# Decode attention on one core: keys in 64 KB rows, a copy on Pool, exponentials in three parts

## The chip, the cores and the metric

The kernel runs on one core of one Trainium2 chip. The time is the device time of one execution in microseconds (us), taken as the median of several runs. The engines are named as the profile does: PE (TensorE, matrix products and transposes), DVE (VectorE), ACT (ScalarE), POOL (GpSimd) and SP (SyncE, which issues most DMA here). PEld is PE's loading of the stationary operand.

## The reference

Two attention layers decode one token for four batch rows. Their outputs stand side by side in the result.

```python
def _A_ref(x, k_cache, v_cache, wq, wo):       # 32 query heads, 8 key/value heads, last 2048 keys only
    W = min(4096, max(256, Sk // 4))           # Sk = 8192, so W = 2048
    q = (x @ wq).reshape(B, Sq, Hq, Dh).transpose(0, 2, 1, 3)
    k = jnp.repeat(k_cache[:, :, Sk - W:, :], rep, axis=1)
    v = jnp.repeat(v_cache[:, :, Sk - W:, :], rep, axis=1)
    p = softmax(einsum("bhqd,bhkd->bhqk", q, k) * Dh ** -0.5)
    o = einsum("bhqk,bhkd->bhqd", p, v)
    return o.transpose(0, 2, 1, 3).reshape(B, Sq, Hq * Dh) @ wo

# _B_ref is the same with 32 key/value heads and all 8192 keys
return concatenate([A, B], axis=-1)            # B = 4, Sq = 1, D = 512, Dh = 128, bfloat16
```

Layer B reads 4 x 32 x 8192 x 128 keys and as many values, 268 MB each. Layer A reads 33.6 MB of keys and values. There is one query per head, so nearly all of the work is to bring the caches in and to pass each key and value through PE once.

## The kernel before

Layer A is done in 8 chunks, then layer B in 32. A B chunk is one batch row and four heads: 256 tiles of 128 keys, 8.4 MB of keys and as many of values. A partition holds 64 KB of a chunk's keys (and 64 KB of its values), contiguous in memory.

On-chip buffers for these lie in one tensor of ten slots of 16 KB per partition. In layer B the keys use slots 0 to 3 and the values slots 4 to 7.

```python
kv = sb("kv", [P, NH, 8192], BF16)              # NH = 10 slots
wol = kv[:, 8, 0:4 * DO].rearrange("p (u n) -> p u n", u=4)
QK = (0, 4, 8, 16, 24)                          # transpose groups that wait for keys
QV = (0, 16, 24, 28, 30, 31)                    # product groups that wait for values
```

Keys come in two halves (32 KB a partition), values in one load, and the last chunks in smaller pieces. A load waits for what reads its slots: a key slot for the last transpose of its quarter, a value slot for the last product. SP issues the loads in this order. Pool waits for each landing and raises a counter (`relay`), on which PE waits.

```python
def dma_B(kind, c, part=None):
    ...
    if kind == "k":
        pieces, fam = (LASTK, "d_lk") if c == NC - 1 else (NEXTK, "d_nk") if c == NC - 2 else ((NTB // 2,) * 2, "d_bk")
    else:
        pieces, fam = (LASTV, "d_lv") if c == NC - 1 else (NEXTV, "d_nv") if c in (NC - 2, NC - 3) else ((NTB,), "d_bv")
    ...
    for i, n in enumerate(pieces):
        waits = []
        for u in range(j0 // unit, (j0 + n - 1) // unit + 1):
            waits += held[at + u]
            used[at + u] = [("T", ch["s"] + (u + 1) * unit // TG - 1) if kind == "k" else ("pv", c)]
        x = slice(j0 * P, (j0 + n) * P)
        sch.add_dma("sp", lambda e, x=x: e.dma_start(dst[:, x], src[:, x]), fam + str(i), waits=waits, key=(kind, c, i))
        j0 += n
        sch.relay("pool", sems, "r_" + kind, n // TG, [(kind, c, i)] + ...)

for c in range(NCA, NC):
    if (c - NCA) % NB == 0:
        dma_B("k", c, 0)
        dma_wos((c - NCA) // NB)                # 0.5 MB of the output weights, every fourth chunk
        dma_B("k", c, 1)
    else:
        dma_B("k", c)
    dma_B("v", c)
```

PE works through a B chunk in three stages. First, 32 groups of 8 tiles are transposed into PSUM (`emit_T`), copied to SBUF by DVE or ACT (22 and 10 groups) and multiplied with the query (`emit_S`). Then come the row maximum and the exponentials, during which PE reorders output weights and runs some dummy products (`keep_busy`). Last, the values are multiplied with the exponentials (`emit_pv`), which ends with the scaling on DVE (`norm_out`).

```python
def exp_B(c):
    for h in range(2):                          # two halves of the keys, four heads each
        for u, pp in HEADS:
            src = sc[pp, h, :].rearrange("p (j u) -> p u j", u=4)[:, u, :]
            dst = probs_of(c)[pp, h * NTB // 2:(h + 1) * NTB // 2, u]
            sch.add("act", lambda e, ...: e.activation(dst, src, ACTF.Exp, bias=negb[pp, 0, u:u + 1], scale=scale), ...)

def whole_B(c):
    emit_qb(c)                                  # DVE copies the chunk's four query columns
    for g in range(ch["NG"]):
        emit_T(ch["s"] + g)
        if g == 1:
            emit_fin(p)                         # output product of the chunk before
        if g >= SLAG:
            emit_S(ch["s"] + g - SLAG)
        ...
    stats_rowmax(c, 1)
    reorder(c, 0, 0)
    reorder(c, 1, 1)
    reorder(c, 2, 2)
    keep_busy(2)
    stats_gmax(c)
    keep_busy(1)
    stats_bc(c)
    exp_B(c)
    for u in range(3):
        take_wol(c, u, u)
    keep_busy(3)
    reorder(c, 3, 0)
    keep_busy(5)
    take_wol(c, 3, 0)
    sums_B(c)
    for g in range(ch["NG"]):
        emit_pv(c, g)
        ...
    norm_out(c)
```

A dummy product is a 128x128 by 128x512 matmul into `po` that nothing reads.

Of the kernel before, what the change touches and what calls it, by code (L numbers as in the profile page):

```python
# [8 lines left out]
AX = mybir.AxisListType  # L9
BF16 = mybir.dt.bfloat16  # L10
F32 = mybir.dt.float32

P = 128
TG = 8
# [154 lines left out]
def bass_concat_heads__sliding_block_cached__mha_block_cached__decode_kernel(  # L169
# [45 lines left out]
    with ExitStack() as es:  # L215
# [51 lines left out]
        semnames += ["d_h%d" % i for i in range(NH)] + ["d_bk0", "d_bk1", "d_bv0"]  # L267
        semnames += [f + str(i) for f, x in (("d_lk", LASTK), ("d_nk", NEXTK), ("d_lv", LASTV), ("d_nv", NEXTV)) for i in range(len(x))]
        semnames += ["d_wo%d" % i for i in range(NWO)] + ["d_wos"]
        sems = {n: es.enter_context(nc.semaphore(n)) for n in semnames}  # L270

# [88 lines left out]
            src = T[:, ch["g"], SkA - W:, :].rearrange("b (pp j) d -> pp b (j d)", pp=P // NB)  # L360
            sch.add_dma("sp", lambda e: e.dma_start(kv[:, at, :], src), "d_h%d" % at, waits=waits, key=(kind, c))

        def dma_B(kind, c, part=None):


            ch = chunks[c]
            T, at, steps = (B_k, KB, QK) if kind == "k" else (B_v, VB, QV)
            src = T[ch["b"], 4 * ch["hq"]:4 * ch["hq"] + 4].rearrange("u (pp j) d -> (u pp) (j d)", pp=P // 4)
            dst = flat(at, 4)
            if kind == "k":  # L370
                pieces, fam = (LASTK, "d_lk") if c == NC - 1 else (NEXTK, "d_nk") if c == NC - 2 else ((NTB // 2,) * 2, "d_bk")
            else:
                pieces, fam = (LASTV, "d_lv") if c == NC - 1 else (NEXTV, "d_nv") if c in (NC - 2, NC - 3) else ((NTB,), "d_bv")
            j0, unit, used = 0, NTB // 4, {}
            for i, n in enumerate(pieces):
                if part is not None and i != part:
                    j0 += n
                    continue
                waits = []
                for u in range(j0 // unit, (j0 + n - 1) // unit + 1):  # L380
                    waits += held[at + u]
                    used[at + u] = [("T", ch["s"] + (u + 1) * unit // TG - 1) if kind == "k" else ("pv", c)]
                x = slice(j0 * P, (j0 + n) * P)
                sch.add_dma("sp", lambda e, x=x: e.dma_start(dst[:, x], src[:, x]), fam + str(i), waits=waits, key=(kind, c, i))
                j0 += n
                sch.relay("pool", sems, "r_" + kind, n // TG, [(kind, c, i)] + ([("wos", ch["hq"])] if i == 1 and kind == "k" and ch["b"] == 0 else []))
            for g, end in zip(steps, steps[1:] + (NTB // TG,)):
                sch.tk[(kind + "r", c, g)] = ("r_" + kind, (c - NCA) * (NTB // TG) + end)
            for u in used:
                held[u] = used[u]  # L390

        KB, VB = 0, 4

        dma_x(0)
        dma_x(1)
# [6 lines left out]
            dma_A("v", c)  # L402
            dma_wo(c)
        for c in range(NCA, NC):
            if (c - NCA) % NB == 0:
                dma_B("k", c, 0)
                dma_wos((c - NCA) // NB)
                dma_B("k", c, 1)
            else:
                dma_B("k", c)  # L410
            dma_B("v", c)

        ms_read = []
        po_read = []
# [42 lines left out]


        def tile_of(kind, c, j):
            at = half_of[(kind, c)] if c < NCA else KB if kind == "k" else VB  # L460
            return flat(at, chunks[c]["NT"] // NTA)[:, j * P:(j + 1) * P]

        bank_used = [None] * NTRB
# [1 line left out]
        def emit_T(s):  # L465
            c, g = groups[s]
            bank = g % NTRB
            if c == NCA and g == 0:
                bank_used[:] = [None] * NTRB
            before, bank_used[bank] = bank_used[bank], s  # L470
            for t in range(TG):
                waits = []
                if t == 0:
                    if c >= NCA:
                        waits = [("kr", c, g)] if g in QK else []
# [115 lines left out]
        def probs_of(c):  # L591
            ch = chunks[c]
            return pbt[ch["ab"]][:, par(c), 0:ch["NT"] * ch["UC"]].rearrange("p (j x) -> p j x", x=ch["UC"])

        def exp_B(c):
            pw = [("c_pb", 1)] + ([("pv", c - 1), ("rs", c - 1)] if c > NCA else [])
            for h in range(2):
                for u, pp in HEADS:
                    src = sc[pp, h, :].rearrange("p (j u) -> p u j", u=4)[:, u, :]
                    dst = probs_of(c)[pp, h * NTB // 2:(h + 1) * NTB // 2, u]  # L600
                    sch.add("act", lambda e, src=src, dst=dst, pp=pp, u=u: e.activation(dst, src, ACTF.Exp, bias=negb[pp, 0, u:u + 1], scale=scale),  # L601
                            waits=[("negb", c)] + pw if u == h == 0 else [], key=("exp", c, h) if u == 3 else None)
                sc_read[h] = [("exp", c, h)]

        def sums_B(c):
            sch.add("dve", lambda e: e.tensor_reduce(out=rst[1][:, :], in_=probs_of(c).rearrange("p j u -> p u j"), axis=AX.X, op=ALU.add),  # L606
                    waits=[("exp", c, 1)] + rs_read[NSM], key=("rs", c))

        def shift_A(c):
            C = chunks[c]["C"]  # L610
# [185 lines left out]
        def whole_B(c):  # L796


            ch, p = chunks[c], prev(c)
            sch.mark()  # L800
            emit_qb(c)
# [116 lines left out]
```

## Time and profile before

| what | before |
|---|---|
| time, median of 3 runs | 1372.56 us (1372.38 to 1374.11) |
| span of the profiled run | 1371.8 us |
| PE busy | 1249.8 us (91%) |
| DVE busy | 744.0 us (54%) |
| ACT busy | 513.8 us (37%) |
| POOL busy | 9.8 us (1%), all at the start |
| read from memory | 587.21 MB |
| granted PE clock over the span | 0.981 |
| transposes `tr<-identb,kv` | 8704 |
| evictions `kt<-tr` on DVE | 736, mean 691 ns |
| exponentials `pbb<-sc,negb` | 256, mean 538 ns |
| dummy products `po<-sel,identb` | 352 |

Busy time of an engine is a share of the whole span and says little of what ends a wait. In the timeline a row gives the start, the duration, the engine, the line, the operation with its shapes and how often it was repeated; the bracket gives the idle time of that engine just before and what ended it. "POOLq" in a bracket stands for Pool's instruction queue, that is, the counter that Pool raises after a landing. A DMA share of 1.00 means that the packets took as much time as 16 engines have.

### The profile page before, as it was taken

The page shows a single profiled execution, that of the slowest core. Times are in us where ns is not written, and L with a number is a line of the kernel's source. Part 1 is how long each engine was busy: PE and PEld are TensorE (multiplying, and loading weights), DVE is VectorE, ACT ScalarE, POOL GpSimd, SP SyncE. Part 2 cuts the span into 40 slices and gives each one's busy share as a digit, 9 for nine tenths or more (in the row PEclk, how much of TensorE's full clock was granted, in tenths as well). Part 3 has the DMA queues.
Part 4 walks back from the last instruction along what each step waited for, and adds up shares of the span by engine and source line. Part 5 has one row for each costly group of instructions (what it writes and reads, how often), then busy time and mean ns, then how long its engine had stood idle before and what let it go on. Part 6 is the DMA issues. An engine that isn't in the chain of part 4 may idle for free.

```text
span 1371.8 us, 61526 instructions
## 1 busy us (share of the span) xinstructions
PE 1249.8 (91%) x27769; PEld 1110.4 (81%) x27769; DVE 744.0 (54%) x1335; ACT 513.8 (37%) x649; POOL 9.8 (1%) x29
## 2 busy tenths in 40 slices
PE   4897999998999999999999999999999999998998
PEld 4786788888778787888777888888778889877887
DVE  1675456655545556555555555554555555554555
ACT  1553244433333344333333443333333433333333
POOL 2000000000000000000000000000000000000000
PEclk9998899999999999999999999999999999999999
DMA  9999999999999999999999999999999999999998
GB/s 398 427 426 444 417 422 431 432 437 441 428 438 428 423 434 434 431 438 440 428 428 424 438 431 429 445 432 428 434 429 429 430 438 438 434 430 429 422 428 340
DMA packets 21084, 587.52 MB, mean 428 GB/s; under 512 B 2356, under 2 KB 2376, under 8 KB 4808
## 3 DMA queue, kind: packets, MB, share of 16 engines
q1 hardware_dynamic: 21032, 587.21, 99.6%
q8 instruction: 15, 0.25, 0.1%
q14 instruction: 5, 0.04, 0.0%
q10 hardware_dynamic: 32, 0.01, 0.0%
HBM read 587.21 MB, written 0.01 MB: 428 GB/s over the span
## 4 chain that ended last, share of the span: by engine, by line
DMA 57%; PE 39%; DVE 2%; issue 1%; ACT 0%; SPq 0%; POOLq 0%; DVEq 0%
DMA kv<-in_B_k_cache_dram 36%; DMA kv<-in_B_v_cache_dram 18%; PE tr L419 18%; PE po L421 9%; PE sc L421 8%; DMA kv<-in_B_wq_dram 2%; PE fin L421 1%; PE ms L421 1%; PE tr L421 1%; DMA kv<-in_A_k_cache_dram 1%; DVE sA L539 1%; DVE kt L486 0%; DVE kv L716 0%; ACT pba L623 0%; DVE rm L551 0%
## 5 line engine op out<-in xcount | busy, mean ns | idle before, releaser
L419 PE MATMUL tr<-identb,kv 128*128 128x128 bf16 x8704 | 668.6, 221 | 48.2 <-POOLq L72 42.3
L486 DVE COPY kt<-tr 128x1024 bf16<-128x1024 bf16 x736 | 501.9, 691 | 264.0 <-PE tr L419 261.3
L484 ACT ACTIVATE kt<-tr 128x1024 bf16<-128x1024 bf16 x352 | 359.3, 1023 | 703.5 <-PE tr L419 703.4
L419 PEld LDWEIGHTS tr<-identb,kv 128*128 128x128 bf16 x8704 | 510.3, 99 | 61.1 <-DVE qq L495 41.2
L421 PE MATMUL sc<-qq,kt 128*128 128x64 bf16 x8192 | 399.3, 192 | 13.5 <-DVE kt L486 9.8
L421 PEld LDWEIGHTS sc<-qq,kt 128*128 128x128 bf16 x8192 | 332.9, 98 | 16.9 <-DVE kt L486 13.1
L421 PEld LDWEIGHTS po<-pbb,kv 128*128 128x128 bf16 x8192 | 250.9, 99 | 37.1 <-issue 20.5
L421 PE MATMUL po<-pbb,kv 128*128 128x64 bf16 x8192 | 253.8, 194 | 24.1 <-POOLq L72 22.6
L601 ACT ACTIVATE pbb<-sc,negb 32x128 bf16<-32x128 f32 x256 | 137.8, 538 | 136.3 <-DVE negb L584 133.0
L421 PE MATMUL po<-sel,identb 128*128 128x512 bf16 x352 | 96.9, 384 | 0.0
L716 DVE CAST kv<-tr 128x512 bf16<-128x512 f32 x128 | 80.0, 683 | 0.0
L606 DVE TENSOR_REDUCE rsb<-pbb 128x4 f32<-128x1024 bf16 x32 | 39.0, 1220 | 65.8 <-ACT pbb L601 65.8
L421 PE MATMUL tr<-wos,back 32*128 32x512 bf16 x512 | 67.8, 383 | 3.2
L421 PEld LDWEIGHTS po<-sel,identb 128*128 128x128 bf16 x352 | 26.6, 98 | 47.6 <-issue 27.8
L668 DVE RECIPROCAL rinv<-ms 128x4 f32<-128x4 f32 (+1 forms) x40 | 7.8, 196 | 105.6 <-PE ms L421 105.6
L555 DVE TENSOR_REDUCE rh<-sc 128x4 f32<-128x512 f32 x64 | 43.9, 686 | 14.3 <-PE sc L421 14.3
L421 PEld LDWEIGHTS tr<-wos,back 32*128 32x128 bf16 x512 | 21.5, 93 | 34.0 <-DVE kv L716 18.9
L690 DVE TENSOR_TENSOR oz<-po,rz 128x16 bf16<-128x16 f32 x32 | 5.6, 175 | 67.9 <-PE po L421 67.9
L570 DVE TENSOR_REDUCE gm<-ms 4x4 f32<-4x128 f32 x40 | 11.2, 279 | 28.6 <-PE ms L419 28.6
L421 PE MATMUL sc<-qb,kt 128*128 128x64 bf16 (+3 forms) x512 | 26.3, 197 | 0.4 <-DVE gx L576 0.4
L421 PEld LDWEIGHTS ms<-gm,ind 4*128 4x128 f32 x64 | 9.4, 182 | 17.5 <-DVE gm L570 17.5
L421 PEld LDWEIGHTS sc<-qb,kt 128*128 128x128 bf16 x512 | 22.1, 102 | 1.6 <-issue 0.9
(65 smaller groups left out, 250.4 us busy)
## 6 DMA issues: line engine op xcount, KB each, us to landing
kv<-in_B_k_cache_dram SPq DMA_DIRECT2D x60, 4096.0 KB, 27.4
kv<-in_A_k_cache_dram SPq DMA_DIRECT2D x8, 2048.0 KB, 13.0
kv<-in_A_v_cache_dram SPq DMA_DIRECT2D x8, 2048.0 KB, 14.6
kv<-in_B_k_cache_dram SPq DMA_DIRECT2D x7, 2048.0 KB, 28.4
kv<-in_B_v_cache_dram SPq DMA_DIRECT2D x3, 4096.0 KB, 22.3
kv<-in_B_v_cache_dram SPq DMA_DIRECT2D x3, 2048.0 KB, 26.8
kv<-in_B_v_cache_dram SPq DMA_DIRECT2D x5, 1024.0 KB, 29.6
kv<-in_A_wq_dram SPq DMA_DIRECT2D x1, 4096.0 KB, 12.5
```

The source lines that it names most:

```text
L419: sch.add("pe", lambda e: e.transpose(o, l, r), waits, key)
L421: sch.add("pe", lambda e: e.matmul(o, l, r, start=start, stop=stop), waits, key)
L484: sch.add("act", lambda e: e.activation(dst, src, ACTF.Copy), waits=waits, key=("ev", s))
L486: sch.add("dve", lambda e: e.tensor_copy(dst, src), waits=waits, key=("ev", s))
L539: emit = lambda e, src=src, b=b: e.scalar_tensor_tensor(out=t, in0=src, scalar=mk[:, b:b + 1], in1=t, op0=ALU.mult, op1=ALU.add)
L555: sch.add("dve", lambda e: e.tensor_reduce(out=rh[:, half, :], in_=src, axis=AX.X, op=ALU.max), waits=[("S", ch["s"] + (half + 1) * ch["NG ...
L570: sch.add("dve", lambda e: e.tensor_reduce(out=gm[0:C, m, 0:U], in_=src, axis=AX.X, op=ALU.max), waits=[("trm", c)], key=("gmax", c))
L601: sch.add("act", lambda e, src=src, dst=dst, pp=pp, u=u: e.activation(dst, src, ACTF.Exp, bias=negb[pp, 0, u:u + 1], scale=scale), waits=[ ...
L606: sch.add("dve", lambda e: e.tensor_reduce(out=rst[1][:, :], in_=probs_of(c).rearrange("p j u -> p u j"), axis=AX.X, op=ALU.add), waits=[( ...
L668: sch.add("dve", lambda e: e.reciprocal(out=ri, in_=ms[:, L0:L0 + n]), waits=[("L", c)], key=("rinv", c))
L690: sch.add("dve", lambda e: e.tensor_tensor(out=o, in0=i0, in1=i1, op=ALU.mult), waits=waits, key=("oT", c))
L716: sch.add("dve", lambda e: e.tensor_copy(wol[:, u, :], o), waits=[("reord", c) if u == 3 else ("reord", c, u)] + [("fin", prev(c))], key=( ...
```

## The change

Each key load of the 26 B chunks from the second on becomes one DMA of whole 64 KB rows into slots 0 to 3. Such a load could not be reissued until all of slots 0 to 3 were free; so Pool copies the second half from slots 2 and 3 to slots 8 and 9 as soon as the load has landed, in four parts, and PE transposes the second half from there. Slots 0 and 1 are free after the first half's transposes, slots 2 and 3 after the copies. The first B chunk and the last five keep pieces, of which the second half goes straight to slots 8 and 9. Some late value loads come in halves too. Output weights of every fourth chunk now follow the keys.

The exponentials come in three parts (a quarter, a quarter, a half), so that the value products can begin after the first quarter, and `keep_busy` shrinks by three dummy products a chunk. The reordered output weights move out of slot 8.

```diff
+HALVES = (128, 128)
-QK = (0, 4, 8, 16, 24)
+QK = (0, 4, 8)
+QC = (16, 20, 24, 28)
...
-        wol = kv[:, 8, 0:4 * DO].rearrange("p (u n) -> p u n", u=4)
+        wol = wor[:, 0, :].rearrange("p (u n) -> p u n", u=4)
...
-        def dma_B(kind, c, part=None):
+        def dma_K(c):
+            ch, i0, half = chunks[c], c - NCA, NTB // 2
+            src = B_k[ch["b"], 4 * ch["hq"]:4 * ch["hq"] + 4].rearrange("u (pp j) d -> (u pp) (j d)", pp=P // 4)
+            T = [("T", ch["s"] + (u + 1) * NTB // 4 // TG - 1) for u in range(4)]
+            wos = [("wos", ch["hq"])] if ch["b"] == 0 else []
+            if c in PIECES_K:
...                                             (pieces: first half to slots KB, second to KX)
+            else:
+                sch.add_dma("sp", lambda e: e.dma_start(flat(KB, 4), src), "d_bk0", waits=held[KB] + held[KB + 1] + held[KB + 2] + held[KB + 3], key=("k", c, 0))
+                if wos:
+                    dma_wos(ch["hq"])
+                sch.relay("pool", sems, "r_k", half // TG, [("k", c, 0)])
+                for k in range(4):
+                    x = slice(k * half // 4 * P, (k + 1) * half // 4 * P)
+                    sch.ops["pool"].append((
+                        lambda e, x=x: e.tensor_copy(flat(KX, 2)[:, x].bitcast(I32), flat(KB + 2, 2)[:, x].bitcast(I32)),
+                        tuple(held[KX + k // 2] + [("k", c, 0)] + (wos if k == 3 else [])), ("r_c", half // 4 // TG), None))
+                held[KB + 2] = held[KB + 3] = [("cp", c)]
+                sch.tk[("cp", c)] = ("r_c", (i0 + 1) * half // TG)
+            held[KB], held[KB + 1], held[KX], held[KX + 1] = [T[0]], [T[1]], [T[2]], [T[3]]
...
+        def dma_V(c):
+            fam, pieces = PIECES_V.get(c, ("d_bv", (NTB,)))
...
+        KB, VB, KX = 0, 4, 8
+        PIECES_K = {NCA: ("d_fk", HALVES), NC - 5: ("d_fk", HALVES), NC - 4: ("d_fk", HALVES),
+                    NC - 3: ("d_nk", NEXTK), NC - 2: ("d_nk", NEXTK), NC - 1: ("d_lk", LASTK)}
+        PIECES_V = {NC - 5: ("d_hv", HALVES), NC - 4: ("d_hv", HALVES), NC - 3: ("d_nv", NEXTV), NC - 2: ("d_nv", NEXTV), NC - 1: ("d_lv", LASTV)}
...
         for c in range(NCA, NC):
...
+            dma_K(c)
+            dma_V(c)
...
+        EXPS = ((0, NTB // 4), (NTB // 4, NTB // 2), (NTB // 2, NTB))
+
         def exp_B(c):
-            for h in range(2):
+            for k in range(3):
+                h, (j0, j1) = EXPS[k][0] * 2 // NTB, EXPS[k]
...
@@ def emit_pv(c, g)
-                if c >= NCA and j == NTB // 2 - NW // 4:
-                    waits = [("exp", c, 1)]
+                for k in (1, 2):
+                    if c >= NCA and j == EXPS[k][0] - NW // 4:
+                        waits = [("exp", c, k)]
...
@@ def whole_B(c)
-            keep_busy(2)
+            keep_busy(1)
...
-            keep_busy(5)
+            keep_busy(3)
```

More of the change, by code (lines that the diff above doesn't have):

```diff
@@ L11 @@
 F32 = mybir.dt.float32
+I32 = mybir.dt.int32
 P = 128
@@ L266, in bass_concat_heads__sliding_block_cached__mha_block_cached__decode_kernel @@
         semnames = ["eng_pe", "eng_dve", "eng_act", "eng_pool", "eng_sp", "d_x0", "d_x1", "d_o0", "d_o1", "r_k", "r_v"]
-        semnames += ["d_h%d" % i for i in range(NH)] + ["d_bk0", "d_bk1", "d_bv0"]
-        semnames += [f + str(i) for f, x in (("d_lk", LASTK), ("d_nk", NEXTK), ("d_lv", LASTV), ("d_nv", NEXTV)) for i in range(len(x))]
+        semnames += ["d_h%d" % i for i in range(NH)] + ["d_bk0", "d_bv0", "r_c"]
+        semnames += [f + str(i) for f, x in (("d_lk", LASTK), ("d_nk", NEXTK), ("d_fk", HALVES), ("d_lv", LASTV), ("d_nv", NEXTV), ("d_hv", HALVES)) for i in range(len(x))]
         semnames += ["d_wo%d" % i for i in range(NWO)] + ["d_wos"]
@@ L361, in dma_A @@
             sch.add_dma("sp", lambda e: e.dma_start(kv[:, at, :], src), "d_h%d" % at, waits=waits, key=(kind, c))
-        def dma_B(kind, c, part=None):
-            ch = chunks[c]
[L367 to L374, printed above, removed]
-            for i, n in enumerate(pieces):
[L376 to L382, printed above, removed]
+        def dma_K(c):
[4 more added lines that the diff above has]
+            if c in PIECES_K:
+                fam, pieces = PIECES_K[c]
+                j0 = 0
+                for i, n in enumerate(pieces):
+                    at = KB if j0 < half else KX
+                    dst = flat(at, 2)[:, (j0 % half) * P:(j0 % half + n) * P]
+                    waits = []
+                    for u in range(j0 % half * 4 // NTB, (j0 % half + n - 1) * 4 // NTB + 1):
+                        waits += held[at + u]
+                    x = slice(j0 * P, (j0 + n) * P)
+                    sch.add_dma("sp", lambda e, x=x, dst=dst: e.dma_start(dst, src[:, x]), fam + str(i), waits=waits, key=("k", c, i))
+                    j0 += n
+                    if wos and j0 == NTB:
+                        dma_wos(ch["hq"])
+                    sch.relay("pool", sems, "r_k" if j0 <= half else "r_c", n // TG, [("k", c, i)] + (wos if j0 == NTB else []))
+            else:
+                sch.add_dma("sp", lambda e: e.dma_start(flat(KB, 4), src), "d_bk0", waits=held[KB] + held[KB + 1] + held[KB + 2] + held[KB + 3], key=("k", c, 0))
+                if wos:
+                    dma_wos(ch["hq"])
+                sch.relay("pool", sems, "r_k", half // TG, [("k", c, 0)])
[7 more added lines that the diff above has]
+            held[KB], held[KB + 1], held[KX], held[KX + 1] = [T[0]], [T[1]], [T[2]], [T[3]]
+            for steps, name in ((QK, "r_k"), (QC, "r_c")):
+                for g, end in zip(steps, steps[1:] + (steps[0] + half // TG,)):
+                    sch.tk[("kr", c, g)] = (name, i0 * half // TG + end - steps[0])
@@ L383, in dma_B @@
+        def dma_V(c):
+            ch = chunks[c]
+            src = B_v[ch["b"], 4 * ch["hq"]:4 * ch["hq"] + 4].rearrange("u (pp j) d -> (u pp) (j d)", pp=P // 4)
+            dst = flat(VB, 4)
+            fam, pieces = PIECES_V.get(c, ("d_bv", (NTB,)))
+            j0 = 0
+            waits = held[VB] + held[VB + 1] + held[VB + 2] + held[VB + 3]
+            for i, n in enumerate(pieces):
                 x = slice(j0 * P, (j0 + n) * P)
-                sch.add_dma("sp", lambda e, x=x: e.dma_start(dst[:, x], src[:, x]), fam + str(i), waits=waits, key=(kind, c, i))
+                sch.add_dma("sp", lambda e, x=x: e.dma_start(dst[:, x], src[:, x]), fam + str(i), waits=waits, key=("v", c, i))
@@ L385, in dma_B @@
                 j0 += n
[L386 to L392, printed above, removed]
+                sch.relay("pool", sems, "r_v", n // TG, [("v", c, i)])
+            for g, end in zip(QV, QV[1:] + (NTB // TG,)):
+                sch.tk[("vr", c, g)] = ("r_v", (c - NCA) * (NTB // TG) + end)
@@ L394, in bass_concat_heads__sliding_block_cached__mha_block_cached__decode_kernel @@
+            for u in range(4):
+                held[VB + u] = [("pv", c)]
+        KB, VB, KX = 0, 4, 8
+        PIECES_K = {NCA: ("d_fk", HALVES), NC - 5: ("d_fk", HALVES), NC - 4: ("d_fk", HALVES),
+                    NC - 3: ("d_nk", NEXTK), NC - 2: ("d_nk", NEXTK), NC - 1: ("d_lk", LASTK)}
+        PIECES_V = {NC - 5: ("d_hv", HALVES), NC - 4: ("d_hv", HALVES), NC - 3: ("d_nv", NEXTV), NC - 2: ("d_nv", NEXTV), NC - 1: ("d_lv", LASTV)}
         dma_x(0)
@@ L404, in bass_concat_heads__sliding_block_cached__mha_block_cached__decode_kernel @@
         for c in range(NCA, NC):
[L405 to L411, printed above, removed]
+            dma_K(c)
+            dma_V(c)
         ms_read = []
@@ L459, in tile_of @@
         def tile_of(kind, c, j):
-            at = half_of[(kind, c)] if c < NCA else KB if kind == "k" else VB
+            if c >= NCA and kind == "k":
+                return flat(KB if j < NTB // 2 else KX, 2)[:, j % (NTB // 2) * P:(j % (NTB // 2) + 1) * P]
+            at = half_of[(kind, c)] if c < NCA else VB
             return flat(at, chunks[c]["NT"] // NTA)[:, j * P:(j + 1) * P]
@@ L474, in emit_T @@
                     if c >= NCA:
-                        waits = [("kr", c, g)] if g in QK else []
+                        waits = [("kr", c, g)] if g in QK + QC else []
                     else:
@@ L593, in probs_of @@
             return pbt[ch["ab"]][:, par(c), 0:ch["NT"] * ch["UC"]].rearrange("p (j x) -> p j x", x=ch["UC"])
+        EXPS = ((0, NTB // 4), (NTB // 4, NTB // 2), (NTB // 2, NTB))
         def exp_B(c):
             pw = [("c_pb", 1)] + ([("pv", c - 1), ("rs", c - 1)] if c > NCA else [])
-            for h in range(2):
+            for k in range(3):
+                h, (j0, j1) = EXPS[k][0] * 2 // NTB, EXPS[k]
                 for u, pp in HEADS:
-                    src = sc[pp, h, :].rearrange("p (j u) -> p u j", u=4)[:, u, :]
-                    dst = probs_of(c)[pp, h * NTB // 2:(h + 1) * NTB // 2, u]
+                    src = sc[pp, h, :].rearrange("p (j u) -> p u j", u=4)[:, u, j0 - h * NTB // 2:j1 - h * NTB // 2]
+                    dst = probs_of(c)[pp, j0:j1, u]
                     sch.add("act", lambda e, src=src, dst=dst, pp=pp, u=u: e.activation(dst, src, ACTF.Exp, bias=negb[pp, 0, u:u + 1], scale=scale),
-                            waits=[("negb", c)] + pw if u == h == 0 else [], key=("exp", c, h) if u == 3 else None)
-                sc_read[h] = [("exp", c, h)]
+                            waits=[("negb", c)] + pw if u == k == 0 else [], key=("exp", c, k) if u == 3 else None)
+                sc_read[h] = [("exp", c, k)]
         def sums_B(c):
             sch.add("dve", lambda e: e.tensor_reduce(out=rst[1][:, :], in_=probs_of(c).rearrange("p j u -> p u j"), axis=AX.X, op=ALU.add),
-                    waits=[("exp", c, 1)] + rs_read[NSM], key=("rs", c))
+                    waits=[("exp", c, 2)] + rs_read[NSM], key=("rs", c))
         def shift_A(c):
```

## The prediction

> **What bounds the kernel now.** I read the page first, then the DMA queue's issues in order of time, then the timeline around the start of a chunk and around the start of its value products, and last the DMA answers for short windows.
>
> ```profile
> DMA  9999999999999999999999999999999999999998
> ...
> DMA packets 21084, 587.52 MB, mean 428 GB/s; under 512 B 2356, under 2 KB 2376, under 8 KB 4808
> ...
> q1 hardware_dynamic: 21032, 587.21, 99.6%
> ...
> DMA 57%; PE 39%; DVE 2%; issue 1%; ACT 0%; SPq 0%; POOLq 0%; DVEq 0%
> ```
>
> From the page: the 16 DMA engines are busy in every slice, 99.6% of the span, while TensorE (PE) has 91%. The chain that ended last alternates between the two. So bytes set the time, and PE follows closely.
>
> ```profile
> 671.05 0.33 SPq L384 DMA_DIRECT2D kv<-in_B_v_cache_dram  x1
> ...
> 671.74 0.17 DVE L495 COPY qq<-qs 128x4 bf16 x1 [0.50 <-issue]
> ...
> 672.88 0.34 PE L419 MATMUL tr<-identb,kv 128*128 128x128 bf16 x3 [1.85 <-POOLq L72]
> ```
>
> ```profile
> 661.26 1.25 PE L421 MATMUL po<-sel,identb 128*128 128x512 bf16 x5
> ...
> 663.18 1.50 PE L421 MATMUL po<-pbb,kv 128*128 128x64 bf16 x46 [0.67 <-POOLq L72]
> ```
>
> These are two places of one B chunk in the timeline (start, duration, engine, line, operation; in brackets the idle time before it and what ended it). The transposes start only when Pool passes on that a key half has landed, after 1.85 us; the value products wait 0.67 us for the values. Chunks start at 672.88, 711.66 and 750.45: the period is 38.78 us. A chunk's 16.78 MB over that is 432.6 GB/s. Where a fourth chunk adds 0.52 MB of output weights the period is 40.05 us (594.05 to 634.10), as the bytes demand.
>
> How much of it is packets? Two windows, one nearly all values (64 KB rows), one mostly keys (32 KB rows):
>
> ```profile
> DMA packets 125, 6.59 MB, mean 412 GB/s; under 512 B 14, under 2 KB 14, under 8 KB 14
> ...
> q1 hardware_dynamic: 125, 6.59, 95.2%
> ```
>
> ```profile
> DMA packets 242, 7.57 MB, mean 445 GB/s; under 512 B 32, under 2 KB 32, under 8 KB 32
> ...
> q1 hardware_dynamic: 242, 7.57, 103.4%
> ```
>
> Bytes over share times window give 6.59 / (0.952 x 16 us) = 432.7 GB/s for values and 7.57 / (1.034 x 17 us) = 430.6 for keys. A least-squares fit of the same two numbers over 130 windows of 8 us (210 to 1250 us) gives 1.217 us for a 32 KB packet and 2.421 us for a 64 KB one. Two small ones thus cost 12.6 ns more than one large one.
>
> PE slows after some of these waits:
>
> ```profile
> 750.45 1.64 PE L419 MATMUL tr<-identb,kv 128*128 128x128 bf16 x16 [1.87 <-POOLq L72]
> 752.02 1.02 PE L421 MATMUL fin<-kv,oz 128*4 128x256 bf16 x8
> 752.97 1.03 PE L419 MATMUL tr<-identb,kv 128*128 128x128 bf16 x8
> ...
> 754.20 0.61 PE L419 MATMUL tr<-identb,kv 128*128 128x128 bf16 x8
> ```
>
> Usually the first 16 transposes take 1.06 us; here they take 1.64, and the pace is back at 754.20. I found four such starts (398.88, 750.45, 790.48, 1142.08) among the twenty or so after an idle of about 1.86 us. Each costs about 1.4 to 1.7 us of PE time.
>
> [...] The trace has only memsets: 1004 ns for 1088 elements and 1912 ns for 2176, 0.83 ns an element whatever its type (512 f32 take 524 ns).
>
> **The change, part by part.**
>
> *Rows.* Of 32 B chunks the first keeps two halves and the last five keep pieces, so 26 chunks load all keys in one DMA. That saves 8 packets on each of 16 engines, 8 x 12.6 ns = 0.10 us a chunk, 2.6 us in all. The values of two late chunks now come in halves and the keys of one in quarters, which gives back about 0.4 us. Net gain 2.2 us.
>
> *Pool copies.* Four copies of 2048 int32 elements; at the memset's rate each is about 1.8 us, all four 7.3 us after the keys land. The second half's transposes start 11.0 us after the chunk's start (672.88 to the next key issue at 683.90) and need the four parts 2.7 us apart. Even at 4 us a copy nobody waits. Copying also frees slots 2 and 3 before that point, so the next key DMA still leaves at 11 us, when the value transfer of some 19.4 us has more than 8 us to go. The copies are off the path.
>
> *The order of landing.* This is the risk. Before, transposes began when the first key half was there, with another 9.7 us of keys still queued when the next values were issued. Now they begin when all keys are there. The next value DMA, issued when the value products end, must be issued before the key transfer runs dry.
>
> *PE's chain.* Where nothing waited (transposes from 1295.71, value issue at 1331.84) a chunk takes 36.13 us. Three dummy matmuls fewer: one ahead of the maximum's transpose, 0.21 us; two ahead of the value products, 0.43 us (three take 0.82 us including the latency, so about 0.21 each). The first values wait for exponentials of a quarter instead of a half: 4 x 0.55 = 2.2 us become about 4 x 0.40 = 1.6 us (an estimate between half and all of 0.55). That is ready just before the dummies end, so it doesn't bind. New chain about 36.13 - 0.64 = 35.5 us, which leaves 38.68 - 35.5 = 3.2 us between value issue and the next chunk's start.
>
> *What must fit into 3.2 us.* The end of the key transfer until PE sees it, plus the time from issue to the first byte of values. The kernel's first load was issued at 0.80 us and used at 13.31; its 8 packets an engine take 9.7 us, so 2.8 us were overhead, of which I put 0.8 on the start-up traffic. With 2.0 us it fits, with 1.2 us to spare.
>
> *The ends.* The first whole load delays PE by some 6 us, but the DMA queue stays full. In the last five chunks, in pieces again, PE catches up 3.2 us a chunk. After the last key wait (1337.94) the rest to 1371.8 us is PE's own chain, and it is 0.5 us shorter.
>
> Sum without a new stall: 1372.6 - 2.2 - 0.5 = 1369.9 us.
>
> **The rivals.** *A: the idle before each chunk cools PE.* The wait grows from 1.86 to 3.2 us, [...] so perhaps half of the chunks start at half clock instead of one in five. Such a chunk needs 35.5 + 1.6 = 37.1 us; then only 1.6 us are left, less than 2.0, and DMA stands still for 0.4 us (1.2 us if the overhead is 2.8). The next chunk then waits less and starts warm, so about 40% would be hit: 26 x 0.4 x (0.4 to 1.2) = 4 to 12 us, that is 1374 to 1382 us. For it: the four slow starts. Against it: a chunk that is hit corrects the next one, and the dummies were cut with this slack in view. *B: Pool is slow or blocked.* Above 4.6 us a copy, the next key issue comes after the value transfer's end and each chunk loses the excess; at 6 us a copy the fourth part ends at 24 us, some 5 us late, x 26 = 130 us. The memset's rate speaks against it. *C: PE becomes the bound through DVE,* [...]: 22 evictions of 691 ns a chunk leave little room. [...] *D: nothing to see,* since the gain is 0.2%.
>
> **Range and chances.** I give half to the clean case (1369 to 1371), three tenths to weak stalls (1371 to 1376), 15% to A in full and 5% to B or C. Predicted: 1371.5 us; 8 times in 10 between 1367 and 1382. [...] Over 2% slower (above 1400 us) needs 1.1 us lost in every chunk: 4%.
>
> **What would show it.** Right: 64 KB key issues of 8 MB, a period of about 38.68 us, DMA share still above 99.5%, four Pool copies of near 1.8 us that end before the second half's transposes, PE idle of about 3.2 us at the chunk's start and none before the value products. A would show as more first transposes at 1.6 us, a granted clock in the steady part below the 0.99 of now, and a DMA share below 99%. B would show as transposes in mid-chunk waiting for Pool, or as late key issues; C as evictions longer than 691 ns. I am wrong on the sign of the steady part if the period is above 38.78 us.

## The result and the profile after

The changed kernel is slower: 1390.2 us, median of 4 runs (1385.1 to 1393.0), against 1372.6 us for the kernel before (4 runs beside it). The ratio is 1.0122, with a 95% interval of 1.0091 to 1.0153. The prediction said 1371.5 us, and 8 times in 10 between 1367 and 1382.

The lines of the page that answer to those shown of before:

```profile
DMA  9999899999999999999999999999999999999998
...
DMA packets 17917, 587.52 MB, mean 423 GB/s; under 512 B 2004, under 2 KB 2024, under 8 KB 4456
...
q1 hardware_dynamic: 17864, 587.21, 98.7%
...
DMA 56%; PE 41%; DVE 1%; issue 1%; SPq 0%; POOLq 0%; DVEq 0%
...
L448 PE MATMUL tr<-identb,kv 128*128 128x128 bf16 x8704 | 679.9, 223 | 93.6 <-POOLq L75 85.0
L517 DVE COPY kt<-tr 128x1024 bf16<-128x1024 bf16 x736 | 502.7, 691 | 321.5 <-PE tr L448 318.7
...
L396 POOL COPY kv<-kv 128x2048 int32<-128x2048 int32 x104 | 192.7, 1898 | 972.0 <-DMA kv<-in_B_k_cache_dram 972.0
...
L450 PE MATMUL po<-pbb,kv 128*128 128x64 bf16 x8192 | 253.7, 194 | 2.4 <-issue 2.4
```

The two lines of before that the waits of PE are read against:

```profile
L419 PE MATMUL tr<-identb,kv 128*128 128x128 bf16 x8704 | 668.6, 221 | 48.2 <-POOLq L72 42.3
...
L421 PE MATMUL po<-pbb,kv 128*128 128x64 bf16 x8192 | 253.8, 194 | 24.1 <-POOLq L72 22.6
```

On the queue of the bulk loads (q1) there are 3168 packets fewer, the bytes are the same, and yet the DMA share fell from 99.6% to 98.7% of a longer span. PE waits 93.6 us in all ahead of transposes (48.2 before), and no longer for values ahead of the products (2.4 us with "issue" as the releaser, that is, no wait that the profile shows; 24.1 before). DVE's evictions still take 691 ns. Pool copies in 1.9 us.

Two stages and two short windows say where DMA stood still. The columns are window, length, busy time and instructions of PE, PEld, DVE, ACT and Pool, then granted PE clock, DMA share and GB/s. Before:

```profile
120.00:200.00 80.00, 71.39 (x1440) 61.48 (x1441) 42.53 (x75) 29.10 (x36) 0.00 (x0) 0.94 1.00 427
200.00:1150.00 950.00, 878.84 (x19719) 782.41 (x19716) 515.37 (x875) 350.98 (x435) 0.00 (x0) 0.99 1.00 433
```

After:

```profile
120.00:200.00 80.00, 70.36 (x1353) 60.76 (x1353) 40.48 (x71) 26.02 (x33) 7.41 (x4) 0.87 0.94 401
200.00:1150.00 950.00, 857.26 (x19221) 772.65 (x19220) 507.76 (x857) 372.51 (x527) 177.87 (x96) 0.97 0.99 426
...
573.00:579.00 6.00, 5.09 (x132) 4.61 (x129) 1.81 (x5) 0.55 (x1) 2.69 (x2) 1.00 0.53 186
614.00:620.00 6.00, 3.00 (x27) 2.21 (x28) 1.38 (x2) 0.00 (x0) 2.95 (x2) 0.53 1.02 437
```

The last two rows are two neighbouring chunk starts. At the first, PE arrives late and DMA moves 186 GB/s for 6 us; at the second, PE is early and idle, cools to a clock of 0.53, and DMA is full. One chunk cools PE, the next pays. The timeline shows that alternation at single chunks:

```profile
1009.22 0.33 SPq L415 DMA_DIRECT2D kv<-in_B_v_cache_dram  x1
...
1010.84 1.06 PE L448 MATMUL tr<-identb,kv 128*128 128x128 bf16 x16 [1.66 <-POOLq L75]
...
1046.39 0.33 SPq L415 DMA_DIRECT2D kv<-in_B_v_cache_dram  x1
...
1050.62 1.37 PE L448 MATMUL tr<-identb,kv 128*128 128x128 bf16 x16 [4.26 <-POOLq L75]
1051.92 1.02 PE L450 MATMUL fin<-wor,oz 128*4 128x256 bf16 x8
1052.87 1.03 PE L448 MATMUL tr<-identb,kv 128*128 128x128 bf16 x8
...
1087.69 0.33 SPq L415 DMA_DIRECT2D kv<-in_B_v_cache_dram  x1
...
1089.36 1.06 PE L448 MATMUL tr<-identb,kv 128*128 128x128 bf16 x16 [1.70 <-POOLq L75]
```

A warm chunk runs from 1010.84 to the value issue at 1046.39, 35.55 us. PE then idles 4.26 us and starts cold (granted clock 0.59 from 1050.62 to 1053.90): the next chunk takes 37.07 us (1050.62 to 1087.69). I call the time from a chunk's value issue to the start of its transposes the *gap*. It is 1.62 us at 1009.22, then 4.23, then 1.67. The period after a short gap is 39.78 us (1010.84 to 1050.62), a loss of 1.0; after the long one 38.74 us.

The sizes of that loss come from the trace. Over the 24 chunks that start between 200 and 1140 us, the periods exceed those of before (38.78, or 40.05 where output weights follow the keys) by 14.6 us in all. Nine chunks lose over 0.5 us and make 14.9 of it. On the DMA side, between 100 and 1350 us the engines, as a mean of the 16, stood idle for 13.8 us (0.7 before). And the 64 KB packets between 215 and 1160 us took 8.3 us an engine longer than their median of 2.418 us would make (0.6 before with both sizes): the slow ones are the first packets of value loads that were issued late, some 3.1 us each, up to 4.1. So 13.1 us idle plus 7.7 us slow, less the 2.2 us that the rows save and the 0.5 us of the tail (both as predicted), is 18.1 us against the 17.6 us by which the profiled span grew.

### The profile page after: what moved, and what is told of

Its sections match the earlier page's. It is cut to its first block, busy times and chain, and to the rows that moved or that the text cites. A ratio compares the mean times of both kernels' runs of the same rounds, so it can differ in the third digit from the quotient of the medians.

```text
span 1389.4 us, 61669 instructions
## 1 busy us (share of the span) xinstructions
PE 1244.8 (90%) x27673; PEld 1116.6 (80%) x27673; DVE 747.0 (54%) x1335; ACT 547.3 (39%) x777; POOL 202.5 (15%) x133
## 3 DMA queue, kind: packets, MB, share of 16 engines
q1 hardware_dynamic: 17864, 587.21, 98.7%
HBM read 587.21 MB, written 0.01 MB: 423 GB/s over the span
## 4 chain that ended last, share of the span: by engine, by line
DMA 56%; PE 41%; DVE 1%; issue 1%; SPq 0%; POOLq 0%; DVEq 0%
DMA kv<-in_B_k_cache_dram 52%; PE tr L448 22%; PE sc L450 10%; PE po L450 5%; DMA kv<-in_A_k_cache_dram 2%; DMA kv<-in_B_wq_dram 2%; PE fin L450 2%; PE tr L450 1%; PE ms L450 1%; DVE kt L517 0%; DVE wor L751 0%; DVE sA L570 0%; DVE gm L601 0%; PE ms L448 0%; DVE rm L582 0%
## 5 line engine op out<-in xcount | busy, mean ns | idle before, releaser
L448 PE MATMUL tr<-identb,kv 128*128 128x128 bf16 x8704 | 679.9, 223 | 93.6 <-POOLq L75 85.0
L448 PEld LDWEIGHTS tr<-identb,kv 128*128 128x128 bf16 x8704 | 520.2, 100 | 108.9 <-issue 87.1
L450 PE MATMUL sc<-qq,kt 128*128 128x64 bf16 x8192 | 402.0, 192 | 13.8 <-DVE kt L517 10.4
L450 PEld LDWEIGHTS sc<-qq,kt 128*128 128x128 bf16 x8192 | 335.7, 99 | 17.5 <-DVE kt L517 13.1
L396 POOL COPY kv<-kv 128x2048 int32<-128x2048 int32 x104 | 192.7, 1898 | 972.0 <-DMA kv<-in_B_k_cache_dram 972.0
L635 ACT ACTIVATE pbb<-sc,negb 32x64 bf16<-32x64 f32 (+1 forms) x384 | 171.1, 445 | 131.5 <-DVE negb L615 126.3
L640 DVE TENSOR_REDUCE rsb<-pbb 128x4 f32<-128x1024 bf16 x32 | 39.1, 1220 | 99.8 <-ACT pbb L635 99.8
L751 DVE CAST wor<-tr 128x512 bf16<-128x512 f32 x128 | 80.1, 684 | 1.2 <-PE tr L450 1.2
L450 PE MATMUL po<-sel,identb 128*128 128x512 bf16 x256 | 77.2, 390 | 0.0
L450 PEld LDWEIGHTS po<-sel,identb 128*128 128x128 bf16 x256 | 19.9, 98 | 39.6 <-issue 28.8
L586 DVE TENSOR_REDUCE rh<-sc 128x4 f32<-128x512 f32 x64 | 43.9, 686 | 14.3 <-PE sc L450 14.3
L450 PE MATMUL fin<-wor,oz 128*4 128x256 bf16 x264 | 25.1, 324 | 0.4 <-DVE oz L725 0.4
## 6 DMA issues: line engine op xcount, KB each, us to landing
kv<-in_A_k_cache_dram SPq DMA_DIRECT2D x8, 2048.0 KB, 14.6
```

The source lines that it names most:

```text
L396: lambda e, x=x: e.tensor_copy(flat(KX, 2)[:, x].bitcast(I32), flat(KB + 2, 2)[:, x].bitcast(I32)),
L448: sch.add("pe", lambda e: e.transpose(o, l, r), waits, key)
L450: sch.add("pe", lambda e: e.matmul(o, l, r, start=start, stop=stop), waits, key)
L586: sch.add("dve", lambda e: e.tensor_reduce(out=rh[:, half, :], in_=src, axis=AX.X, op=ALU.max), waits=[("S", ch["s"] + (half + 1) * ch["NG ...
L751: sch.add("dve", lambda e: e.tensor_copy(wol[:, u, :], o), waits=[("reord", c) if u == 3 else ("reord", c, u)] + [("fin", prev(c))], key=( ...
```

## The experiments

Three theories stood. *Theory 1*: the next values are issued too late for a queue that holds only one key load, and idle that cools PE makes every second chunk late. *Theory 2*: the order of landing alone does it, without cooling. *Theory 3*: the cut of the dummies does it. (Some of the expectations word Theory 2 anew.) "Steady loss" below is the sum named above, periods over 38.78 or 40.05 us for chunks that start between 200 and 1140 us.

### PE kept warm, three ways

*fill12* and *warm* add twelve dummy products behind a chunk's last product, so that PE is busy while it waits. They stand after the value issue's condition and don't delay it, but they can delay the transposes that follow them.

```diff
             norm_out(c)
+            if NCA < c < NC - 6:      # fill12;  warm: if c < NC - 6
+                fill(c, 12)           # 12 dummies, 128x128 by 128x512, into a free bank of sc
```

The last six chunks then differ from the rest, so PE's program has one more loop; in *warm* that loop is placed like the second one.

> The changed kernel with twelve dummy products more (about 2.6 us) behind the last value product of each whole-load chunk, so that PE isn't idle while it waits for the next keys; nothing waits for them but the next transposes. Theory 1 (the wait cools PE, a cooled chunk issues its values late, and the shortened DMA queue runs dry): PE stays warm, granted clock 0.98 or more, DMA share 99.3% or more, value issue 35.5 us after the chunk's start every time, 1370 to 1376 us. Theory 2 (the queue runs dry by the order of landing alone, warm or not): clock back, time still above 1384. Theory 3 (the dummies that were cut inside the chunk are what is missing): still above 1384 and PE cold in the exponential stage.

*fill12* took 1430.2 us, ratio 1.0424 (1.0398 to 1.0451): far above the 1370 to 1376 us of Theory 1, and of little use for telling the theories apart. Its steady loss is 8.3 us, near that of *warm* below. The rest is at the seams of the loops: in the profile, PE idles with "issue" as the releaser, as two rows of the timeline show.

```profile
1205.82 1.59 PE L450 MATMUL po<-pbb,kv 128*128 128x64 bf16 x49 [2.49 <-issue]
...
1252.90 1.89 PE L448 MATMUL tr<-identb,kv 128*128 128x128 bf16 x16 [6.92 <-issue]
```

What PE waits for at these seams, no run shows.

> The changed kernel with twelve dummies behind every whole-load chunk's products, [...]. Theory 1 (cooling is the whole cause): 1370 to 1374 us and a period of 38.7 us. Theory 2 amended (a warm chunk of 35.5 us leaves only 3.2 us, and about that is needed from the first engine's last key packet until PE starts, 1.3 us, plus from the value issue until its first packets run at full pace, 1.7 to 2.0 us; so even warm chunks lose a little): a period of about 39.1 us as in the loop part of the first such run, 1378 to 1383 us, granted clock 0.98 or more.

*warm* took 1390.2 us, ratio 1.0129 (1.0100 to 1.0159), no better than the change as a whole. But by stage it is better, as the windows show:

```profile
120.00:200.00 80.00, 68.68 (x1362) 60.33 (x1362) 39.68 (x69) 25.80 (x32) 7.40 (x4) 0.94 1.01 435
200.00:1150.00 950.00, 910.05 (x19703) 790.34 (x19703) 512.13 (x869) 378.23 (x539) 177.72 (x96) 0.99 1.00 429
1150.00:1250.00 100.00, 93.79 (x2122) 84.97 (x2118) 53.58 (x91) 38.12 (x52) 7.41 (x4) 0.98 0.94 400
```

The clock is back at 0.99 and the steady loss falls from 14.6 to 6.6 us, a mean period of 39.1 us without output weights, as Theory 2 amended expected. Between 1150 and 1250 us, where the last loop begins, it gives back: one period there is 41.95 us (35.43 in the kernel after), with "issue" waits of 1.59 and 1.16 us. So keeping PE warm takes away about half of the steady loss, but not all. Starts behind a warm chunk still lose: two at a gap of 3.16 us lost 1.16 and 1.71 us. The rest isn't purely that of a warm PE, though: three of the 24 chunks still took 37.1 us to the value issue, and at the starts behind them the transposes followed the dummies without a wait, so that the dummies held them up.

*warm_ch5* lengthens PE's chain ahead of the value issue by 1.07 us (five dummies before the last eight products); *warm_pv28* shortens it by 0.96 us, by leaving out the last 32 of a chunk's 256 value products (its output lacks them), with 16 dummies instead of twelve.

```diff
             for g in range(ch["NG"]):
+                if g == 31 and c < NC - 6:
+                    fill(c, 5)                                   # warm_ch5
-            for g in range(ch["NG"]):
+            for g in range(ch["NG"] - 4 if c < NC - 6 else ch["NG"]):   # warm_pv28
```

> The same with five dummies more ahead of the last 8 value products, so the value issue comes 1.07 us later in each of 26 chunks. Theory 2 amended, with its recurrence (a stall in one chunk gives the next one as much slack, so half of a delay is paid): 14 us more than the kernel without these five, 1392 to 1397. If a delay is paid in full: 28 us more. If the queue is still deep enough (theory 1): no more than 3 us more.

> The opposite direction: the same warm kernel without the last 32 of 256 value products in each whole-load chunk (this part of the sum is left out) and with sixteen dummies instead of twelve behind them, so the value issue comes 0.96 us earlier while PE works as long. Theory 2 amended: the queue never runs dry, no first packet is slowed, period 38.68 us, 1369 to 1372 us. If the time of the longer rows were taken by something else (Pool's copies, the longer transfers), it stays where the kernel with all products is.

They took 1409.3 us (1.0257; 1.0240 to 1.0274) and 1384.1 us (1.0068; 1.0050 to 1.0087), with steady losses of 22.3 and 4.0 us (6.6 in *warm*). Both times hold a seam as well (one period of 45.78 and of 46.46 us), so the steady losses say more: with PE mostly warm, 1.07 us more on the chain costs 15.7 us, and 0.96 us less gains 2.6. Not all of the 15.7 is the late value issue. Where the transposes follow the dummies without a wait, the periods of *warm_ch5* are 39.01 to 39.03 us, so PE's own work, dummies included, is there longer than the 38.7 us that the bytes take. *warm_pv28* misses both outcomes that were named for it: the loss shrinks, but doesn't end. What the two show is the sign: a longer chain loses more and a shorter one less, which Theory 3 doesn't say.

### The dummies put back

*kb_back* is the kernel after with the dummies of before.

```diff
-            keep_busy(1)
+            keep_busy(2)
...
-            keep_busy(3)
+            keep_busy(5)
```

> The changed kernel with its three dummy products put back (2 and 5 as before). Theory 1: the first B chunk is warm again in its exponentials (about 5 us back), the later ones have 0.64 us less idle and as much less slack, so 1380 to 1388 us. Theory 2: the longer chain costs half of 0.64 us in each of 26 chunks, 1394 to 1400. Theory 3: 1375 or less.

1389.2 us, ratio 1.0119 (1.0100 to 1.0139): 1.2 us above what Theory 1 gave, and outside the other two. The first chunk recovers: from 150 to 200 us the clock is 0.93 (0.86 after) and DMA moves 422 GB/s (381). The steady loss stays at 14.3 us. Theory 3 falls for all but the first chunk.

### The two halves of the change, each alone

*pe_only* is the kernel before with the exponentials in three parts and the three dummies fewer; *rows_only* is the kernel after with exponentials and dummies as before, so that only rows, copies and the order of loads are new.

```diff
-            for h in range(2):                                   # pe_only, on before
+        EXPS = ((0, NTB // 4), (NTB // 4, NTB // 2), (NTB // 2, NTB))
+            for k in range(3):
...
-        EXPS = ((0, NTB // 4), (NTB // 4, NTB // 2), (NTB // 2, NTB))   # rows_only, on after
+        EXPS = ((0, NTB // 2), (NTB // 2, NTB))
```

> The kernel before with only the PE part of the change: exponentials in three parts and three dummies fewer; keys in halves as before. Theory 1: PE idles 0.6 us longer at each chunk's start and cools more often (clock below 0.981), but 9.7 us of keys still lie in the queue, so 1371 to 1374 us. Theory 2: the same. Theory 3: 1380 or more.

> The kernel after with the exponentials in halves and the dummies as before: only the rows, the copies and the order of loads are changed. Theory 1 (the value load is issued too late for a queue that holds only one key load): PE's chain is again some 0.6 us longer, so the lead is shorter still: 1387 to 1395 us, DMA share below 99%, periods that alternate. Theory 3 (the cut of the dummies is what cools PE and loses the time): 1370 to 1375 us.

*pe_only*: 1372.2 us, ratio 0.9996 (0.9987 to 1.0005), periods of 38.78 us. A chain 0.6 us shorter is worth nothing where bytes set the time, and the fewer dummies cost nothing, although the granted clock over the span is 0.970 (0.981 before). *rows_only*: 1389.5 us, ratio 1.0131 (1.0095 to 1.0167), steady loss 12.6 us, as Theory 1 expected. The loss is wholly in this half of the change: rows, copies and order of loads, of which the next runs say more.

### The value load issued earlier

*v_early* leaves everything of the change but cuts each value load into halves, each issued when the products that read its half are done. *v_192* and *v_224* cut at 192 and 224 of the 256 tiles.

```diff
-            fam, pieces = PIECES_V.get(c, ("d_bv", (NTB,)))
-            waits = held[VB] + held[VB + 1] + held[VB + 2] + held[VB + 3]
+            fam, pieces = PIECES_V.get(c, ("d_hv", HALVES))      # v_192: (192, 64)  v_224: (224, 32)
             for i, n in enumerate(pieces):
+                waits = [the product of chunk c - 1 that is the last to read this piece's tiles]
```

> The changed kernel with all values in two halves, each issued as soon as its own half's products are done, so the first half's issue comes about 4 us earlier; values then have 32 KB rows. Theory 1: the queue no longer runs dry although PE is still cooled (clock 0.97 or less, some first transposes still at 1.6 to 1.9 us), DMA share 99.4%, 1371 to 1376 us. Theory 2: the same time. Theory 3: 1385 or more.

*v_early*: 1372.4 us, median of 20 runs (1372.1 to 1373.8), ratio 0.9993 (0.9986 to 0.9999). The whole loss is gone. From its page, the queue of the bulk loads (packets, MB, share of the 16 engines):

```profile
q1 hardware_dynamic: 21752, 587.21, 99.7%
```

From its timeline, the start of one chunk (the two value pieces stand in one row):

```profile
947.09 4.28 SPq L417 DMA_DIRECT2D kv<-in_B_v_cache_dram  x2
...
955.53 1.89 PE L450 MATMUL tr<-identb,kv 128*128 128x128 bf16 x16 [4.52 <-POOLq L75]
```

From its windows, the steady part:

```profile
200.00:1150.00 950.00, 866.73 (x19563) 783.50 (x19585) 517.68 (x873) 379.13 (x540) 177.84 (x96) 0.97 1.00 432
```

PE idles 4.52 us and starts cold here (1.89 us for the first 16 transposes, 1.06 in a warm chunk); the granted clock of the stage is 0.97, as in the kernel after. Yet DMA stands at 1.00, and every period between 200 and 1140 us is within 0.04 us of 38.78 or 40.05. The first half of the values leaves 8.4 us before the transposes start (947.09 to 955.53). So cooling alone costs no time, nor do Pool's copies or the whole key loads, which are all still there: what costs is the value load that comes too late.

> The kernel after with each whole value load cut into 224 + 32 tiles; the first piece is issued when 224 of the 256 products are done, 0.96 us earlier, the rest when all are. Theory 1: the lead grows by 0.96 us of the 2 to 3 us that a cooled chunk lacks: warm chunks fit, cooled ones still stall by about 0.5 us, in every second chunk: a loss of 4 to 8 us is left, 1374 to 1380 us, mean period 38.9 to 39.1. Theory 2 (it is enough that the next values stand in the queue as more than one load, however late): 1371 to 1373 us.

> The same with 192 + 64 tiles: the first piece leaves 1.9 us earlier than the whole load did. Theory 1: nearly every start fits, cooled ones too: 1371.5 to 1374 us, periods of 38.78, PE as cool as in the kernel after. Theory 3 (cooling of PE costs the time by itself): 1385 us or more in both cuts.

*v_224*: 1385.1 us, ratio 1.0079 (1.0050 to 1.0107). *v_192*: 1379.7 us, ratio 1.0048 (1.0026 to 1.0070). Both lie above what Theory 1 expected. Two loads in the queue aren't enough by themselves (Theory 2 as worded there), and the cool PE alone doesn't cost 1385 us in both, as *v_192* shows (Theory 3). The time falls in step with the lead (how much earlier the first piece is issued). All three kernels with cut loads have 21752 packets on the bulk queue, so their number isn't what sets them apart. The steady part of *v_224* in the windows:

```profile
200.00:1150.00 950.00, 860.68 (x19301) 778.01 (x19323) 514.22 (x865) 374.04 (x528) 177.87 (x96) 0.96 0.99 427
```

The same of *v_192*:

```profile
200.00:1150.00 950.00, 863.26 (x19354) 778.95 (x19378) 516.65 (x870) 377.13 (x537) 177.71 (x96) 0.97 1.00 429
```

PE's clock is about as low in both (0.96 and 0.97) as in the kernel after (0.97), while the bytes move at 427 and 429 GB/s (426 after, 432 in *v_early*). The four kernels with a cool PE make a series (the loss is that of the profiled run, the time the median of all runs):

| first value piece | issued earlier by | steady loss | time |
|---|---|---|---|
| whole load (after) | 0 | 14.6 us | 1390.2 us |
| 224 tiles | 0.93 us | 11.2 us | 1385.1 us |
| 192 tiles | 1.87 us | 6.6 us | 1379.7 us |
| 128 tiles | 3.95 us | 0.0 us | 1372.4 us |

The gap shows why I had expected too little. Over the chunks of after, *kb_back*, *rows_only*, *v_224*, *v_192* and *v_early* that start between 200 and 1140 us (those without output weights between keys and values), sorted by the gap. "DMA idle" is the mean of the 16 engines around the start, "slow packets" what the bulk packets there took beyond their usual time, as a mean of the engines:

| gap, first value issue to the chunk's transposes | chunks | mean loss in the period that follows | DMA idle | slow packets |
|---|---|---|---|---|
| under 2 us | 20 | 1.61 us | 1.52 us | 0.66 us |
| 2 to 3 us | 11 | 1.30 us | 0.47 us | 0.59 us |
| 3 to 4 us | 16 | 0.35 us | 0.06 us | 0.27 us |
| 4 to 5 us | 20 | 0.09 us | 0.01 us | 0.13 us |
| over 5 us | 41 | 0.02 us | 0.00 us | 0.06 us |

In the mean a start needs a gap of 4 us and more to cost next to nothing. Single starts differ: between 2 and 3 us they lose from nothing to 2.7 us. The kernels with dummies behind the products are left out, since there the dummies move the starts too. Where 0.5 MB of output weights stands in the queue between keys and values, a gap under 2 us costs only 0.15 us (16 chunks): those 1.3 us of other bytes do the same service.

A cold chunk in *v_192* still ends with a gap of 2.3 to 3.9 us, within the range that loses. I had put the need at the start of the first packets only, about 3 us.

No version beats the kernel before by more than *v_early*'s 0.07%. It spends on cut value loads what the key rows save, and its periods are the 38.78 us of before.

## Why the prediction was wrong

*What bounds it, and that no gain above 2.2 us was to be had*: right as far as it can be seen. The five shortest periods without output weights between 200 and 1140 us are 38.65 to 38.74 us in the kernel after (38.68 said); no run's total shows the gain. At the 432.6 GB/s of the kernel before, 587.21 MB take 1357 us, an estimate: a kernel of that rate throughout would be 1.1% faster.

*Pool copies off the path*: right. 1898 ns each (1.8 us said), 7.4 us for four; DVE's evictions keep their 691 ns (B and C fall); *v_early* has the copies and loses nothing.

*PE's chain of 35.5 us*: right. 35.42 us in the last chunks, 35.55 in the warm chunk above; the wait for values is gone.

*The order of landing*: named as the risk, and it is the cause.

***What must fit into 3.2 us*: the step that failed.** It put 2.0 us for the end of the key transfer until PE sees it plus the start of the values, and 1.2 us to spare. The term is mis-sized. What a start needs is some 4 us, by the table; at 3 to 4 us, where a warm chunk of 35.5 us puts it, 0.35 us is lost already in the mean. The trace names the parts. The 16 engines don't end the key load together: their completions are spread over 0.5 to 1.0 us at 18 of the 24 starts and over 2.0 to 3.2 us at the other 6, and PE starts 0.5 to 0.7 us after the last packet. At the other end, a value packet starts no sooner than 0.96 us after its issue, and the pace of the first packets went with how far ahead of the first engine's last keys the issue came. At the 18 starts without output weights, the first 16 packets of 64 KB took 2.42 to 2.45 us in the mean where it came 2.4 us or more ahead, 2.50 to 2.80 us at 1.3 to 1.8 us, and 2.90 to 3.20 us below 1 us. So some 2 us ahead is what they needed here. Added up (2 us, the spread, and 0.5 to 0.7), that is an estimate of 3.0 to 3.7 us at the 18 starts with the small spread and of 4.5 us and more at the 6. The first load of the kernel before, from which I took 2.8 us, shows the same parts. Its first packet starts 1.05 us after the issue, its first 16 packets of 32 KB take 1.93 us in the median (1.22 in the steady part), and the completions are spread over 0.74 us. The 0.8 us that I took off as start-up traffic is about what the slow first packets make. I should have kept the larger figure; it leaves 0.4 of the 3.2 us, while the spread at 6 starts is wider than that load's by 1.2 us and more. The 0.96 us to the first packet isn't yet the time to the full rate.

*Rival A*: the mechanism is right in each step (longer idle, cold chunks, a chunk that is hit corrects the next), and so is its count: 9 of 24 chunks lose over 0.5 us, 38% (40% said). The count fits in part by chance: 14 of the 24 chunks are cold and take 36.8 us or more to the value issue (half were said, by my estimate), but only 8 of them are followed by such a loss. Its size is wrong: 1.0 to 2.7 us a hit (0.57 once), 1.66 in the mean, where it had 0.4 to 1.2. That is the same mis-sized term, 2.0 or 2.8 us instead of some 4. With the measured 1.66 us it makes 26 x 0.4 x 1.66 = 17 us on top of 1369.9, that is 1387 us against the measured 1390.2. That a cold PE runs at about half clock is measured: at two of the four cold starts of before the granted clock is 0.54 (398.88 to 402.60 and 750.45 to 754.20), in the kernel after it is 0.59 from 1050.62 to 1053.90, and the eight transposes at 1052.87 take 1.03 us (0.61 warm). How long an idle cools PE is not shown: the four cold starts of before came after waits of only 1.84 to 1.87 us, as long as those of most of its warm starts. *v_early* shows that the low clock alone costs no time here.

*The ends*: "the DMA queue stays full" at the first whole load was wrong for the kernel after. PE was cold there (clock 0.87 from 120 to 200 us), so that the second chunk's values left at 174.41 us, after its transposes had begun (174.22), and the engines idled 4.5 us in the mean between 150 and 200. With the dummies back (*kb_back*) the values left at 170.65, 2.9 us ahead, and the engines idled 1.1 us: the one place where Theory 3 holds. Three of the last chunks caught up 3.2 us each, as said (periods of 35.42); the next two waited for keys again (1.65 and 1.24 us) and took 37.17 and 36.76. From the last key wait to the end it is 33.86 us before (1337.94 to 1371.8) and 33.24 after (1356.16 to 1389.4): 0.6 us less, where 0.5 was said.

## What to carry to other kernels

When a transfer is merged or reordered, work out for each load how far ahead it will be issued of the moment at which the running transfer's consumer can start, and don't be content with the bare latency. In this kernel the 0.96 us to the first packet were not enough: it took 4 us (some 3.4 us ahead of the last packet's end), and below that, engines idled and the first packets ran slow. A queue that held another load gave that lead with little or no loss (half of the values: 0.0 us in all; 0.5 MB of weights: 0.15 us a start); a wait at the head of the queue on the last consumer of a whole buffer took it away (14.6 us in all). Where the lead was short, a consumer's chain that had grown longer, by a PE cooled in its own wait (35.55 us warm, 37.07 cold), turned into lost time on the DMA engines, here in 9 of 24 steps.

## What was not expected of the hardware

- In the kernel after, the first packets of a value load issued less than 1 us before the first engine was through with its keys, with no output weights between, took about 3.1 us (up to 4.1) instead of 2.42 us for 64 KB. Why is open: no run separates the start of the load from what else the engines do then. The kernel's first load, with nothing ahead of it in its queue, began slowly too (1.93 us instead of 1.22 for 32 KB).
- With twelve or sixteen dummies behind a chunk, and so one loop more in PE's program, 5 us and more were lost at the seams (periods of 41.95 in *warm* and waits of 6.92 us in *fill12*), with the releaser "issue". What PE waits for there is not shown.
- Runs of kernels with this loss scatter more: 1385 to 1393 us for after, 1386 to 1397 for *rows_only*, against 1372.1 to 1373.8 for *v_early*. The kernel before lies between the two (1372.3 to 1377.4). The cause of the scatter is not shown.
